# Splitting the broadcast of a block's softmax reciprocals into four transfers of one row each

## The chip, the core and the metric

The kernel runs on one core of a Trainium2 chip. A core has five instruction queues that run side by side and meet only through semaphores: TensorE (PE, matrix products, with its weight loads shown as PEld), VectorE (DVE), ScalarE (ACT), GpSimd (POOL) and SyncE (SP), which here does nothing but issue DMA transfers. Sixteen DMA engines carry the transfers. The metric is device time in microseconds; lower is better.

## The reference

One input x of 2048 rows and 512 columns is normalised row by row. The normalised xn goes through two branches, whose results are added to x: attention with 32 heads of width 16, and a gated feed-forward of inner width 1792.

```python
xn = layernorm(x)
q, k, v = split(xn @ wqkv)                      # 32 heads of width 16
scores = einsum("bhqd,bhkd->bhqk", q, k) * 16 ** -0.5
p = softmax(scores)                             # over the 2048 keys
a = einsum("bhqk,bhkd->bhqd", p, v) -> [2048, 512] @ wo
gate, up = xn @ W_gate, xn @ W_up
b = ((gate * (gate > 0)) * up) @ W_down
out = x + a + b
```

The softmax is not normalised before the product with v. The kernel forms exponentials, multiplies them with v and, in the same product, with a column of ones; that column gives each query's sum. The result is then multiplied by the reciprocal of the sum. The change concerns how these reciprocals reach the partitions where they are needed.

## The kernel before

**Blocks.** Attention runs in 32 blocks. A block is one group of 512 queries (`c4`, four of them), one group of eight heads (`gg`, four of them) and one half of that group (`ee`), so it holds four heads. Within a block the keys are taken in 16 tiles of 128. A product of keys and queries for a block's tile goes to PSUM; the exponential is taken either on ScalarE (L1418, two heads at a time, into `ring`) or, for the tiles marked in `QUAD_AT`, by an integer construction on VectorE and POOL (L1373, L1388, L1392, into `qd`). TensorE multiplies either with `v_aug` and adds the 16 tiles up in one PSUM bank. The feed-forward's products, the projections and the output rows are placed between the attention work.

**The end of a block** is the function `normalise`. The block's number is `n = 8 * c4 + 2 * gg + ee`; the last block has an ending of its own, so 31 blocks take this way:

1. VectorE copies the finished bank to `o_sb` (L1251; the very first block is summed in two parts, L1256). The four heads lie on 32 partitions each, and one of those partitions holds the sums of 512 queries.
2. SyncE issues the fetch of the four rows of sums, reshaped to 128 partitions of 16 (L1267, `rsum`, stream `n1`).
3. VectorE takes the reciprocal (L1268, `rrec`).
4. SyncE issues the write of the reciprocals to a scratch tensor in HBM, `rec_scr[n]`, four rows of 512 (L1269, stream `n2`).
5. SyncE issues the broadcast (L1272, `rb`, stream `n3`): row j of the scratch is read 32 times into partitions 32 j to 32 j + 31, in one transfer of 256 KB.
6. POOL multiplies `o_sb` by `rb` (L1280, or L1285 with four small transfers, L1289, that pack the second half's result into the place beside the first half's). The products with `wo` read the result, `oT`.

`rsum`, `rrec`, `rb` and `o_sb` each have two buffers, used in turn.

**Order.** Every engine's instructions stand in one fixed order. It was made ahead of time and is stored in the kernel as the compressed list `PLAN`; `Graph.run` reads it, and `Graph.emit` writes each engine's queue in that order and puts in the semaphore waits that the data flow requires. Nothing overtakes: when SyncE's next transfer waits for a semaphore, all transfers behind it wait too, and the same holds for a VectorE instruction that waits. Among what shares SyncE's queue with the steps above are slices of `qT` copied from `qf` (L892), slices of the feed-forward's weights (L1044), the rows of x for the residual (L1099), the stores of finished rows (L1118) and the packing transfers (L1289).

**Semaphores.** Each transfer belongs to a stream with a semaphore of its own, and adds 16 to it when it has landed. `emit` gives the transfer's consumers the value to wait for, `16 * (o.val + 1)`, where `o.val` counts earlier transfers of the stream; stream `n3` has four semaphores, used by the blocks in turn. At the end, SyncE waits for each stream's last value (`fin`).

## Time and profile before

| | us |
|---|---|
| median of three runs | 680.99 |
| lowest and highest | 680.63, 682.62 |
| the profiled execution, its own time | 681.0 |
| its span, from the first to the last instruction | 678.1 |

The granted TensorE clock is 1.000 throughout. HBM traffic is 26.35 MB read and 2.35 MB written, 42 GB/s over the span, and the transfers' packets took 17.3% of what sixteen DMA engines could give.

Views used below: the page's busy time of each engine; the chain of work that ended last, in order of time (start, length, what); timelines of one engine (start, length, instruction, and in brackets the idle time before it with what ended it); the view of one tile's instructions (duration in ns: min/median/max, then the first and last start); waits (who waited for whom: us in total, times, longest); and busy times of a stretch. A transfer's own instruction on SyncE, marked SPq, shows how long the *issue* took. The landing, where the profile knows it, stands apart as the time from issue to landing.

### The profile page before, as it was taken

What the parts mean: (1) busy time and instruction counts of PE and PEld (TensorE: products, weight loads), DVE (VectorE), ACT (ScalarE), POOL (GpSimd) and SP (SyncE); (2) the same over time, 40 slices, a digit from 0 to 9 for tenths busy, and PEclk for the clock granted to TensorE, in tenths of its full rate; (3) what the DMA queues carried; (4) which work ended last, traced back from release to release, by engine and by line L of the source; (5) the groups of instructions that cost most, each with busy time, mean ns of one, the idle gap of its engine ahead of it and who ended that gap; (6) DMA issues with size and microseconds to landing.
All of it is one profiled execution on the core that took longest, in us unless ns stands there. A gap on an engine that the chain in (4) does not pass through costs nothing.

```text
span 678.1 us, 46986 instructions
## 1 busy us (share of the span) xinstructions
PE 668.2 (99%) x22358; PEld 392.7 (58%) x21562; DVE 615.1 (91%) x1042; ACT 657.9 (97%) x718; POOL 511.7 (75%) x519
## 2 busy tenths in 40 slices
PE   8999999999999999989999999999999999999998
PEld 3555555566656666555555656555665565565554
DVE  9957899999999999889999989999999899999795
ACT  6999999999999999989999999999999999999995
POOL 3313657877788787888788878888888968888982
PEclk9999999999999999999999999999999999999999
DMA  7321221123121111111111112011112212101121
GB/s 218 66 50 29 60 68 44 47 66 93 47 85 35 48 28 54 39 47 47 51 49 34 52 30 59 17 40 40 58 28 73 61 33 72 39 23 38 33 64 58
DMA packets 55947, 35.97 MB, mean 53 GB/s; under 512 B 19336, under 2 KB 51784, under 8 KB 55752
## 3 DMA queue, kind: packets, MB, share of 16 engines
q1 hardware_dynamic: 55464, 32.71, 17.3%
q8 instruction: 171, 2.80, 1.7%
q10 hardware_dynamic: 288, 0.26, 0.1%
q14 instruction: 24, 0.20, 0.1%
HBM read 26.35 MB, written 2.35 MB: 42 GB/s over the span
## 4 chain that ended last, share of the span: by engine, by line
PE 91%; DVE 5%; DMA 2%; POOL 1%; issue 0%; SPq 0%; ACT 0%; DVEq 0%; POOLq 0%
PE ps L263 91%; DVE qd L1373 1%; DVE stats L758 1%; DVE xn_sb L771 1%; DMA rsum<-o_sb 1%; DMA xnT<-xn_sb 1%; POOL qd L1388 0%; DVE v_aug L909 0%; DMA rec_scr<-rrec 0%; DMA x_sb<-in_A_x_dram 0%; DVE qd L1392 0%; DVE qT L985 0%; DVE kT L902 0%; DVE mv L759 0%; DVE xnT L812 0%
## 5 line engine op out<-in xcount | busy, mean ns | idle before, releaser
L1418 ACT ACTIVATE ring<-ps 128x1024 bf16<-128x1024 f32 x706 | 651.4, 1079 | 6.2 <-PE ps L263 5.3
L1388 POOL TENSOR_TENSOR qd<-qd,ints 128x512 int32<-128x512 int32 x458 | 462.0, 1039 | 131.3 <-DVE qd L1392 81.0
L263 PE MATMUL ps<-qT,kT 64*32 64x512 bf16 x8192 | 466.6, 374 | 3.5 <-DVE qd L1373 2.4
L1373 DVE TENSOR_SCALAR qd<-ps 128x512 int16<-128x512 f32 x636 | 412.3, 684 | 36.2 <-PE ps L263 32.3
L263 PE MATMUL ps<-qd,v_aug 64*32 64x512 bf16 x3816 | 310.3, 375 | 0.1
L263 PE MATMUL ps<-ring,v_aug 64*32 64x512 bf16 x2824 | 244.2, 375 | 0.0
L1353 PEld LDWEIGHTS <-kT 64*32 64x32 bf16 x8032 | 170.9, 92 | 101.7 <-issue 15.5
L1325 PEld LDWEIGHTS <-v_aug 64*32 64x32 bf16 x6004 | 144.8, 92 | 71.8 <-issue 11.2
L263 PE MATMUL ps<-xnT,wgs 64*32 64x512 bf16 x1792 | 140.5, 374 | 0.2 <-DVE qd L1373 0.2
L263 PE MATMUL ps<-xnT,wus 64*32 64x512 bf16 x1792 | 137.3, 375 | 0.4 <-issue 0.2
L1392 DVE TENSOR_SCALAR qd<-qd 128x2048 int16<-128x2048 int16 x89 | 61.9, 701 | 1.2 <-PE ps L263 0.8
L842 PEld LDWEIGHTS <-wus 64*32 64x32 bf16 x1792 | 44.1, 91 | 23.7 <-issue 4.9
L842 PEld LDWEIGHTS <-wgs 64*32 64x32 bf16 x1792 | 43.2, 91 | 22.9 <-issue 3.8
L263 PE MATMUL ps<-Wd,hT 64*32 64x512 bf16 x608 | 55.3, 375 | 0.1
L842 PEld LDWEIGHTS <-hT 64*32 64x32 bf16 x1440 | 35.2, 92 | 21.1 <-issue 4.2
L263 PE MATMUL ps<-Wo_p,x_sb 64*32 64x512 bf16 x480 | 44.8, 375 | 0.0
L1057 DVE COPY up_sb<-ps 128x512 f32<-128x512 f32 x56 | 38.4, 686 | 3.4 <-PE ps L263 3.0
L263 PE MATMUL ps<-Wv,hT 64*32 64x512 bf16 x448 | 41.3, 375 | 0.0
L263 PE MATMUL ps<-Wv,xnT 64*32 64x512 bf16 x576 | 36.7, 374 | 0.5 <-DVE v_aug L909 0.3
L263 PE MATMUL ps<-xnT,Wq 64*32 64x512 bf16 x480 | 37.1, 375 | 0.0
L263 PE MATMUL ps<-xnT,Wk 64*32 64x512 bf16 x480 | 35.8, 374 | 0.3 <-DVE xnT L812 0.3
L263 PE MATMUL ps<-Wk,hT 64*32 64x512 bf16 x384 | 35.8, 375 | 0.0
(73 smaller groups left out, 306.5 us busy)
## 6 DMA issues: line engine op xcount, KB each, us to landing
rb<-rec_scr SPq DMA_DIRECT2D x31, 256.0 KB
wus<-in_B_W_up_dram SPq DMA_DIRECT2D x38, 128.0 KB, 2.9
wgs<-in_B_W_gate_dram SPq DMA_DIRECT2D x38, 128.0 KB, 2.7
xr_sb<-in_A_x_dram SPq DMA_DIRECT2D x16, 128.0 KB, 3.1
qT<-qf SPq DMA_DIRECT2D x120, 16.0 KB, 2.8
out_dram<-xn_sb SPq DMA_DIRECT2D x14, 128.0 KB, 3.2
x_sb<-in_A_x_dram SPq DMA_DIRECT2D x8, 128.0 KB, 2.8
x_sb<-oT SPq DMA_DIRECT2D x60, 16.0 KB, 3.0
```

The source lines that it names most:

```text
L263: return e.add_instruction(mybir.InstMatmult(name=e.bass.get_next_instruction_name(), engine=mybir.EngineType.PE, ins=[e.lower_ap(x), e.lo ...
L758: G.op("DVE", 580, lambda e, m=m: e.bn_stats(stats[:, m, :], xs(m)), reads=[t_xm[m]], writes=[t_st], prio=pr, order=last_xn if m == 4 else ())
L771: G.op("DVE", 320, lambda e, m=m, t=t_n: e.tensor_scalar(xn_sb[:, t.slot, :], xs(m), mv[:, m, 0:1], rstd[:, m:m + 1], op0=ALU.subtract, op ...
L842: e.ldweights(w()[rows, 32 * j:32 * j + 32], tile_position=(rows.start, 32 * j))
L1057: G.op("DVE", 603, lambda e: e.tensor_copy(up_sb[:, tup.slot, :], bank_of(tu)), reads=[tu], writes=[tup], prio=-590)
L1325: e.ldweights(vs(j), tile_position=(64 * half, 32 * j))
L1353: e.ldweights(ks(m), tile_position=(64 * half, 32 * m))
L1373: G.op("DVE", 601, lambda e, j=j, tx=tx: e.tensor_scalar(qd[:, tq.slot, 512 * j:512 * j + 512], ps[:, BANK[tx.slot], :], IBIAS[3], 0.0, op ...
L1388: G.op("POOL", POOL_NS / POOL_PIECES + 60, lambda e, x=x, n=n, c=slice(i * m, i * m + m): e.tensor_tensor(x().bitcast(I32)[:, c], raw().bi ...
L1392: G.op("DVE", 600, lambda e, n=n, x=x: e.tensor_scalar(x(), raw(), float(SHIFTS[n + 1]), None, op0=ALU.add), reads=[ti, tq], writes=[t], p ...
L1418: exp_ops[u] = G.op("ACT", 904, lambda e, tr=tr, k0=k0: e.activation(ring[:, tr.slot, :, :], ps[:, 4 * k0:4 * k0 + 2, :], ACTF.Exp, scale= ...
```

## The change

The broadcast of step 5 becomes a list of four transfers, one for each row j: `rec_scr[n, j]` to the 32 partitions from 32 j on, 64 KB each. They stand at the place in SyncE's order where the one transfer stood, one behind the other, and share its semaphore. The wait for `rec_scr` stands ahead of the first. Each piece adds 16 when it lands, so the value that consumers and the end of the kernel wait for on stream `n3` is 64 for a broadcast in place of 16. The order of all engines, every other transfer and all arithmetic stay as they were.

```diff
+PIECES = {"n3": 4}
...
                 if e == "SP":
-                    o.sem = (dsem[o.stream], 16 * (o.val + 1))
+                    o.sem = (dsem[o.stream], 16 * PIECES.get(o.stream[0], 1) * (o.val + 1))
...
-        fin = [(dsem[s], 16 * n) for s, n in streams.items()]
+        fin = [(dsem[s], 16 * PIECES.get(s[0], 1) * n) for s, n in streams.items()]
...
                 ins = o.fn(eng)
                 if e == "SP":
-                    ins.then_inc(o.sem[0], 16)
+                    for piece in ins if isinstance(ins, list) else [ins]:
+                        piece.then_inc(o.sem[0], 16)
...
-            dma(lambda e: e.dma_start(rb[:, trb.slot, :], rec_scr[n].unsqueeze(1).to_broadcast([4, 32, 512])), 520,
+            dma(lambda e: [e.dma_start(rb[32 * j:32 * j + 32, trb.slot, :], rec_scr[n, j:j + 1, :].to_broadcast([32, 512])) for j in range(PIECES["n3"])], 520,
                 reads=[tsc], writes=[trb], prio=pr - 50, stream=("n3", n % 4), name="n3")
```

## The prediction

> **What bounds the kernel now.** I began with the page: which engine is full, what the last chain consists of, and what the profile says of the broadcast's transfers.

> ```profile
> span 678.1 us, 46986 instructions
> PE 668.2 (99%) x22358; PEld 392.7 (58%) x21562; DVE 615.1 (91%) x1042; ACT 657.9 (97%) x718; POOL 511.7 (75%) x519
> PE 91%; DVE 5%; DMA 2%; POOL 1%; issue 0%; SPq 0%; ACT 0%; DVEq 0%; POOLq 0%
> ...
> rb<-rec_scr SPq DMA_DIRECT2D x31, 256.0 KB
> ...
> out_dram<-xn_sb ACTq DMA_DIRECT2D x2, 128.0 KB, 1.7
> ```

> TensorE is busy for 99% of the span and is 91% of the chain that ended last. A transfer can therefore matter only where it makes TensorE stand still, and the 2% of DMA in the chain is where to look. Note also that the 31 broadcasts have no time to landing in their row; what they take must be found in another way. The second view is the chain in order of time, around the only stretch after the start in which it leaves the compute engines for several microseconds.

> ```profile
> 282.45 2.74 DMA rec_scr<-rrec
> 285.21 0.58 SPq L1272
> 285.84 0.47 SPq L1118
> ...
> 286.35 4.72 DMA rsum<-o_sb
> ...
> 291.95 56.75 PE ps L263 x1763
> ```

> Here the broadcast of one block (L1272) is on the path by its issue: 0.58 us on SyncE's queue, then a store's issue, then the fetch of the **next** block's row sums (L1267), which takes 4.72 us to arrive. The timelines of VectorE and TensorE show what that costs:

> ```profile
> 288.28 0.68 DVE L1373 TENSOR_SCALAR qd<-ps 128x512 int16<-128x512 f32 x1
> 291.10 0.25 DVE L1268 RECIPROCAL rrec<-rsum 128x16 f32<-128x16 f32 x1 [2.14 <-DMA rsum<-o_sb]
> 291.95 0.38 PE L263 MATMUL ps<-qT,kT 64*32 64x512 bf16 x4 [1.98 <-DVE qd L1373]
> ```

> VectorE runs in a fixed order. The reciprocal waits 2.14 us for its row sums, the score patterns behind it (L1373) are late, and TensorE stands for 1.98 us. The same fetch with no broadcast ahead of it is much quicker; the two rows of another block, from SyncE's and VectorE's timelines, give a bound:

> ```profile
> 179.10 0.59 SPq L1267 DMA_DIRECT2D rsum<-o_sb  x1
> 181.41 0.24 DVE L1268 RECIPROCAL rrec<-rsum 128x16 f32<-128x16 f32 x1
> ```

> The reciprocal starts there 181.41 - 179.10 = 2.31 us after the fetch was issued, without waiting; so the fetch alone takes at most 2.31 us. Behind a broadcast it took 4.72. Why the broadcast holds it up is in the busy shares of two stretches (last two columns: share of the 16 DMA engines, GB/s), the second starting 1.65 us after a broadcast's issue:

> ```profile
> 402.75 0.58 SPq L1272 DMA_DIRECT2D rb<-rec_scr  x1
> ...
> 8.00:10.00 2.00, 1.92 (x49) 1.38 (x53) 2.00 (x6) 1.49 (x3) 0.00 (x0) 1.00 1.02 324
> 404.40:405.60 1.20, 1.20 (x56) 0.57 (x44) 0.88 (x3) 1.20 (x3) 1.20 (x2) 1.00 0.26 102
> ```

> During the opening loads all sixteen engines are busy and move 324 GB/s. While the broadcast is moving, the share is 0.26, which is 4.2 engines of 16, and the rate 102 GB/s. So the 256 KB (262,144 bytes) of one broadcast take about 262/102 = 2.57 us, on four engines. The excess of the late fetch, 4.72 - 2.31 = 2.4 us, is about that.

> **The change part by part.** *Data.* A piece is 64 KB, from one row to 32 partitions. If it runs on all sixteen engines at the opening's rate it takes 65.5/324 = 0.20 us. The fetch behind it then meets no queue worth counting, and I take it at 2.31 us, the bound above; the shorter end is 1.7, the quickest landing that any group of transfers shows on the page (the two stores from ScalarE's queue, whose row stands above), the longer end the 4.72 it has now.

> [...]

> *Issue.* SyncE issues four instructions instead of one. What they cost is bounded by the view of each tile's instructions (duration in ns, min/median/max):

> ```profile
> L1272 SPq DMA_DIRECT2D rb<-rec_scr x31: 528/578/598, 76.8 to 661.8; - x31
> L1267 SPq DMA_DIRECT2D rsum<-o_sb x31: 543/593/687, 58.7 to 656.2; - x31
> L1099 SPq DMA_DIRECT2D xr_sb<-in_A_x_dram x16: 336/472/1056, 73.1 to 662.4; - x16
> L892 SPq DMA_DIRECT2D qT<-qf x120: 507/584/1777, 40.8 to 638.2; - x120
> ```

> The nearest row is the load of xr_sb, also from HBM to SBUF in plain rows: median 0.47 us. With 0.04 us between issues (285.21 + 0.58 to 285.84 above leaves 0.05) four take 4 x 0.47 + 3 x 0.04 = 2.00 us in place of 0.58: **1.42 us more** of SyncE's queue. The ends are 4 x 0.34 + 0.12 = 1.48 (0.9 more) and 4 x 0.58 + 0.12 = 2.44 (1.9 more). But there is a catch in the last column. The broadcast and the row-sum fetch never took over 0.69 us to issue, while other kinds take up to 1.06 and 1.78 now and then. The pieces may join the kinds that can be held up. Around the spot that matters such an issue stands in SyncE's timeline:

> ```profile
> 286.99 0.76 SPq L1044 DMA_DIRECT2D wgs<-in_B_W_gate_dram  x1
> ```

> It is 0.3 us above the 0.47. I add one such delay, and take 1.42 + 0.3 = 1.7 us at the decisive place.

> *The place at 286.* The fetch goes out at 286.35 + 1.7 = 288.05 and its reciprocal starts at 288.05 + 2.31 = 290.36 instead of 291.10: 0.74 us earlier, and TensorE, which waits 1.98 us behind it, with it. With the ends above: 286.35 + 0.9 + 1.7 = 288.95 is before VectorE is free (288.28 + 0.68 = 288.96), so all of the 1.98 is gained; with 1.9 + 2.31 the gain is 0.54; and with 4.72 there is a loss.

> *The second place.* VectorE waits for row sums just once more: the first row, from the view of waits, gives the total, the number and the longest (us, times, us). The other four are from SyncE's and VectorE's timelines:

> ```profile
> DVE rrec L1268 <- DMA rsum<-o_sb: 2.5, 2, 2.1
> 515.59 0.58 SPq L1272 DMA_DIRECT2D rb<-rec_scr  x1
> 516.77 0.57 SPq L1267 DMA_DIRECT2D rsum<-o_sb  x1
> ...
> 520.30 0.68 DVE L1057 COPY up_sb<-ps 128x512 f32<-128x512 f32 x1
> 521.34 0.25 DVE L1268 RECIPROCAL rrec<-rsum 128x16 f32<-128x16 f32 x1 [0.36 <-DMA rsum<-o_sb]
> ```

> The pieces end at 515.59 + 2.0 + 0.3 = 517.9, the fetch is back by 517.9 + 0.04 + 2.31 = 520.25, before VectorE is free at 520.98. The 0.36 us goes; TensorE shows no wait beside it, so I count 0.1.

> *The consumer.* The multiply (L1280, L1285, on POOL) needs all four pieces. The last is issued 3 x 0.51 = 1.53 us after the first. Loads to x_sb land in 2.8 us at the median on the page's issue rows, those to xr_sb in 2.0 to 4.8. So rb is there 4.3 us after the first issue (3.5 to 6.3). The tightest use I found:

> ```profile
> 189.27 0.58 SPq L1272 DMA_DIRECT2D rb<-rec_scr  x1
> 194.17 1.28 POOL L1280 TENSOR_TENSOR x_sb<-o_sb,rb 128x512 bf16<-128x512 f32 x1
> x_sb<-in_A_x_dram SPq DMA_DIRECT2D x8, 128.0 KB, 2.8
> DMA to landing us min/median/max: 2.0/3.1/4.8
> ```

> That is 4.90 us, above 4.3. At the long end the multiply is 1.4 us late; POOL then uses up part of the idle time that it now spends waiting for VectorE. I count nothing.

> *Everything queued behind.* Thirty-one broadcasts add 31 x 1.42 = 44 us of issuing (53 with 1.7 each). Behind them in SyncE's order stand slices of qT, weight slices, stores and the next block's fetches. I cost their delay at nothing, because SyncE itself waits at most of these steps and so catches up:

> ```profile
> SPq L1269 <- DVE rrec L1268: 53.6, 15, 10.6
> POOL qd L1388 <- DVE qd L1392: 81.0, 61, 15.6
> ```

> The first of these waits alone is 53.6 us. Where no such wait stands between, as at 286, the cover is gone, and each microsecond of issue is a microsecond for what is behind.

> *Sum.* -0.74 - 0.1 = -0.8 us on the profiled execution's own 681.0 us (span 678.1, 2.9 around it), which is also the median of the three runs, 680.99. **Forecast 680.2 us.** A measurement of this kernel tells about 0.3%, 2.0 us, from no change; so the forecast is "no difference that can be told".

> **Rivals.** *Full gain.* The pieces issue at 0.34 to 0.43 us and no long one falls at 286: both waits vanish, -1.98 - 0.36 = -2.3, 678.7 us. For it speaks the minimum of the xr_sb row, against it that its median is 0.47.

> *SyncE's issues take over* (slower). The row sums are now behind four issues. The gain at 286 is used up once they take 291.10 - 2.31 - 286.35 = 2.4 us more than now, that is 0.72 us a piece: from there on the wait only grows. If all four take the 1.06 us of the xr_sb row's maximum, they need 4.36 us, 3.8 more; the reciprocal is at 286.35 + 3.8 + 2.31 = 292.46 (+1.36), and at the second place at 515.59 + 4.36 + 0.04 + 2.31 = 522.30 (+0.96): +2.3, and as much again if a further pair of blocks loses its cover: 683.3 to 685.6, say 684. For it: the maxima of three issue rows; against it: the medians, and SyncE's long waits.

> *The broadcast lands no sooner* (slower). Either the pieces stay on few engines, so that the change does not do what it says, or sixteen engines reading one 2 KB row get no more than the 102 GB/s of now. Then the fetch still takes 4.72 us and starts 1.42 to 1.9 later: +1.42 to 1.9 at 286, and at 516 the start moves by 0.8 to 1.3 (0.6 us of gap takes the rest): +2.2 to +3.2, 683.2 to 684.2. For it: no row here shows sixteen engines on one source row; against it: the first loads reach 324 GB/s.

> [...]

> **How the numbers follow.** Forecast 0.45 (its own range 679.4 to 681.5), full gain 0.17, SyncE's issues 0.25, no sooner landing 0.13. The range must reach the full gain below and the middle of both slower cases above: 678.7 to 684.6. Faster by over 0.3% (below 679.0) comes from the full gain, 0.17; slower from the two slow rivals less the share that stays under 683.0, 0.36; the rest, 0.47, is within.

> **What would show it.** In the changed kernel's profile the rows of L1272 should count 124, and now carry a time to landing near 2.8 us; the share of the DMA engines after a broadcast should be a short burst, no stretch of 0.26. Their median should be near 0.47 us, with some over 1. VectorE's wait for the row sums near 286 should fall from 2.14 to about 1.4 us, TensorE's from 1.98 to about 1.2, and the one at 521 vanish. I am wrong if new waits of TensorE appear behind a reciprocal, if POOL comes to wait for rb in many blocks, or if the chain shows SyncE's queue in more blocks than now.

## The result, and the profile after

| | us |
|---|---|
| before, median of 11 runs | 682.25 (678.39 to 684.23) |
| after, median of 11 runs | 677.22 (675.67 to 679.42) |
| after over before, 95% interval | 0.9938 (0.9918 to 0.9958) |
| the profiled execution after, its own time and its span | 677.22, 675.0 |

The changed kernel is 0.62% faster, about 4 us, where 0.8 us was forecast, and its time lies under the predicted range. Executions more than 1.5% above the fastest of the same kernel are left out of every ratio, mean and count below: three of 105 of the kernel before and one of its copy. The page of the profile after, its span, the busy times, the shares of the last chain and the row of the broadcast's transfers:

```profile
span 675.0 us, 47079 instructions
PE 666.8 (99%) x22358; PEld 389.3 (58%) x21562; DVE 615.3 (91%) x1042; ACT 656.7 (97%) x718; POOL 512.1 (76%) x519
PE 84%; ACT 6%; DVE 5%; DMA 2%; SPq 1%; issue 0%; POOL 0%
rb<-rec_scr SPq DMA_DIRECT2D x124, 64.0 KB, 2.2
```

There are 93 instructions more, three for each of 31 blocks. The broadcasts now have a time to landing, 2.2 us at the median for a piece. The chain still passes through one broadcast only, that of block 10. Its parts around there, in order of time (start, length, what):

```profile
282.09 1.86 DMA rec_scr<-rrec
...
283.97 0.33 SPq L1274
...
284.34 1.53 SPq L1274
...
285.92 0.43 SPq L1274
...
286.39 0.42 SPq L1274
...
286.85 0.42 SPq L1120
...
287.32 1.88 DMA rsum<-o_sb
```

Four issues stand where one stood, 0.33, 1.53, 0.43 and 0.42 us long. One of them was held up by 1.1 us; the forecast had put 0.3 us there for such a delay. The fetch of the next block's row sums then takes 1.88 us, not 4.72. VectorE's timeline and TensorE's view of waits (us in total, times, longest) show what is left of the wait:

```profile
289.22 0.25 DVE L1270 RECIPROCAL rrec<-rsum 128x16 f32<-128x16 f32 x1 [1.41 <-DMA rsum<-o_sb]
```

```profile
PE ps L264 <- DVE qd L1375: 1.4, 2, 1.2
```

VectorE's wait fell from 2.14 to 1.41 us, TensorE's from 1.98 to 1.24. The prediction also expected short bursts of all sixteen DMA engines. One piece stands alone in this stretch (busy times, then clock, share of the DMA engines, GB/s):

```profile
284.90:285.40 0.50, 0.50 (x28) 0.27 (x16) 0.30 (x1) 0.50 (x2) 0.00 (x0) 1.00 0.35 123
```

That is 62 KB in 0.5 us, at a mean of 5.6 engines' worth. It is a burst, and more than the 4.2 engines of the whole broadcast, but neither sixteen at a time (the highest share in any 0.05 us of it is 0.68, 10.9 engines) nor the 0.20 us that the prediction took for a piece.

At the second place nothing is left. SyncE's and VectorE's timelines there:

```profile
512.64 2.92 SPq L1274 DMA_DIRECT2D rb<-rec_scr  x4
515.60 0.60 SPq L1269 DMA_DIRECT2D rsum<-o_sb  x1
```

```profile
518.25 0.68 DVE L1059 COPY up_sb<-ps 128x512 f32<-128x512 f32 x1
518.85 0.24 DVE L1270 RECIPROCAL rrec<-rsum 128x16 f32<-128x16 f32 x1
```

The reciprocal follows the copy with no bracket behind it, so its row sums were there. The view of the tile `rb` (issue in ns, then POOL's idle time before its multiplies, then the landing):

```profile
L1274 SPq DMA_DIRECT2D rb<-rec_scr x124: 303/422/1762, 77.4 to 660.4; - x124
...
its engine sat idle before it (us, times) until:
  DVE qd L1394: 5.4, 5
...
DMA to landing us min/median/max: 1.9/2.2/3.6
```

POOL does not wait for `rb` at all in this execution. So the waits that the prediction gave for the place at 286 are in the profile, to within 0.1 us. One of its signs of being wrong is there as well: SyncE's queue is on the last chain at a second place, behind the broadcast that follows the one at 512.64. Two rows of the chain, and the wait of TensorE that ends it:

```profile
526.05 0.51 SPq L894
...
526.60 3.74 DMA x_sb<-oT
```

```profile
PE ps L264 <- DMA x_sb<-oT: 0.3, 1, 0.3
```

There a packing transfer is late, and it costs TensorE 0.3 us. The two profiles differ by 3.1 us of span, however, and 0.74 of that is the wait. The rest is what the experiments are about.

### The profile page after: what moved, and what is told of

Same layout as the page of the kernel before. It is cut to its first block, busy times and chain, and to the rows that moved or that the text cites. A ratio compares the mean times of both kernels' runs of the same rounds, so it can differ in the third digit from the quotient of the medians.

```text
span 675.0 us, 47079 instructions
## 1 busy us (share of the span) xinstructions
PE 666.8 (99%) x22358; PEld 389.3 (58%) x21562; DVE 615.3 (91%) x1042; ACT 656.7 (97%) x718; POOL 512.1 (76%) x519
## 4 chain that ended last, share of the span: by engine, by line
PE 84%; ACT 6%; DVE 5%; DMA 2%; SPq 1%; issue 0%; POOL 0%
PE ps L264 84%; ACT ring L1420 6%; DVE stats L760 1%; DVE qd L1375 1%; DVE xn_sb L773 1%; DMA x_sb<-oT 1%; DMA xnT<-xn_sb 1%; DVE v_aug L911 0%; SPq L1274 0%; SPq L1046 0%; DMA x_sb<-in_A_x_dram 0%; DMA rsum<-o_sb 0%; DMA rec_scr<-rrec 0%; DVE qT L987 0%; DVE kT L904 0%
## 5 line engine op out<-in xcount | busy, mean ns | idle before, releaser
L1355 PEld LDWEIGHTS <-kT 64*32 64x32 bf16 x8032 | 169.0, 92 | 102.4 <-issue 14.4
## 6 DMA issues: line engine op xcount, KB each, us to landing
wus<-in_B_W_up_dram SPq DMA_DIRECT2D x38, 128.0 KB, 2.8
wgs<-in_B_W_gate_dram SPq DMA_DIRECT2D x38, 128.0 KB, 2.5
xr_sb<-in_A_x_dram SPq DMA_DIRECT2D x16, 128.0 KB, 3.1
out_dram<-xn_sb SPq DMA_DIRECT2D x14, 128.0 KB, 1.9
x_sb<-in_A_x_dram SPq DMA_DIRECT2D x8, 128.0 KB, 2.5
```

Of the source, the lines that this page charges most:

```text
L1355: e.ldweights(ks(m), tile_position=(64 * half, 32 * m))
```

## The experiments

All times below are medians of the chip that ran the kernel, and ratios are against runs of the kernel before, of the same chip, with their 95% intervals. The kernel before took 686.44 us on the first chip, 687.5 on the second, 688.55 on the third and 687.26 on the fourth; differences are therefore taken within one chip only.

### Which of the 31 broadcasts matters

The first kernel splits the broadcasts of blocks 10 and 22 alone, those behind which the two waits stood. The second splits all but these two.

```diff
+            def spread(e):
+                if not whole:
+                    return [e.dma_start(rb[32 * j:32 * j + 32, trb.slot, :], rec_scr[n, j:j + 1, :].to_broadcast([32, 512])) for j in range(PIECES["n3"])]
+                return e.dma_start(rb[:, trb.slot, :], rec_scr[n].unsqueeze(1).to_broadcast([4, 32, 512]))
+            whole = n not in (10, 22)          # the second kernel: n in (10, 22)
```

> Only the broadcasts of blocks 10 and 22 go out as four pieces, the two behind which VectorE waited for the next block's row sums; the other 29 stay whole. If the whole gain of the change comes from these waits (theory W), this is as fast as the change: ratio to before 0.994. If only the part that the profile shows at that place comes from there (the shift of TensorE at 292 us in the two profiles, 0.73 us) and the rest from all broadcasts (theory F: while a broadcast holds four DMA engines for 2.6 us, instruction transfers for TensorE start late and it runs dry for 0.3 to 0.8 us now and then), the ratio is about 0.999 (-0.75 us).

> The complement: all broadcasts in four pieces except those of blocks 10 and 22. Theory W: no gain, ratio 1.000, and VectorE's 2.1 us wait near 289 us as in before. Theory F: the wait stays, yet most of the gain is there, ratio about 0.995 (-3.4 us), and TensorE's weight loads wait less for instructions (the 'issue' waits: 47 us in before, 44 with the change).

Two blocks: 683.91 us, ratio 0.996 (0.9937 to 0.9984). All others: 684.95 us, 0.9967 (0.9938 to 0.9996). Both gain, and neither gains all. The second kernel keeps both waits for the row sums and is faster than before nonetheless, so part of the gain seems to lie away from them; its interval ends just below 1, so this run alone does not prove it. Its profile showed something else. The view of waits, and then busy times around its second wait (the last three columns are the granted TensorE clock, the share of the DMA engines, GB/s):

```profile
DVE rrec L1270 <- DMA rsum<-o_sb: 5.1, 2, 2.8
PE ps L264 <- DVE qd L1380: 4.0, 3, 2.0
```

```profile
526.00:527.00 1.00, 0.00 (x0) 0.00 (x0) 0.62 (x2) 0.29 (x1) 0.76 (x1) 1.00 0.00 0
527.00:528.00 1.00, 0.77 (x20) 0.33 (x20) 0.77 (x2) 0.00 (x0) 1.00 (x2) 0.91 0.09 8
528.00:529.00 1.00, 1.00 (x24) 0.32 (x16) 0.55 (x1) 0.08 (x1) 0.51 (x1) 0.50 0.38 111
529.00:530.00 1.00, 1.00 (x32) 0.42 (x24) 0.83 (x3) 0.94 (x1) 0.00 (x0) 0.50 0.51 168
530.00:531.00 1.00, 1.00 (x32) 0.39 (x24) 0.61 (x2) 0.40 (x1) 0.00 (x0) 0.50 0.61 174
531.00:532.00 1.00, 1.00 (x40) 0.45 (x32) 0.46 (x1) 0.72 (x2) 0.00 (x0) 0.88 0.47 150
```

TensorE stands still for 1.97 us, starts again at 527.2, and then its clock is **halved** until about 531.2. The clock lost is 0.09 + 3 x 0.50 + 0.12 = 1.7 us, nearly as much as the wait itself. The wait at 292, of 1.86 us, has no such stretch behind it in this execution. The profiles of before and after could not show it: both ran at 1.000.

### The shape of the split

One kernel makes four transfers of 128 columns, each of all four rows to all 128 partitions: four pieces again, but on few engines (at block 10 its share of the DMA engines was 0.27 to 0.30, where the whole broadcast's was 0.26, in the stretch from 404.4 us on). The other makes eight pieces, half a row's partitions each.

```diff
-            dma(lambda e: [e.dma_start(rb[32 * j:32 * j + 32, trb.slot, :], rec_scr[n, j:j + 1, :].to_broadcast([32, 512])) for j in range(PIECES["n3"])], 520,
+            dma(lambda e: [e.dma_start(rb[:, trb.slot, 128 * j:128 * j + 128], rec_scr[n, :, 128 * j:128 * j + 128].unsqueeze(1).to_broadcast([4, 32, 128])) for j in range(PIECES["n3"])], 520,
```

```diff
-PIECES = {"n3": 4}
+PIECES = {"n3": 8}
...
+            dma(lambda e: [e.dma_start(rb[16 * j:16 * j + 16, trb.slot, :], rec_scr[n, j // 2:j // 2 + 1, :].to_broadcast([16, 512])) for j in range(PIECES["n3"])], 520,
```

> Four transfers per broadcast as in the change, but each takes 128 columns of all four rows, so that four rows stay outermost. If the number of engines is what counts (theories W and F both), the data still sits on four engines, the fetch of row sums still queues behind it and starts about 2 us later: slower than before by 2 to 4 us, ratio 1.003 to 1.006. If the gain came from several small transfers as such (theory S), it is as fast as the change, 0.994.

> [...] Expected: slower than the change by 2 us, ratio to before 0.997; and if SyncE's queue is near its limit in many blocks (the rival that I forecast), 1.003 or more.

Columns: 683.63 us, 0.9962 (0.9936 to 0.9988), a gain; the loss expected of it did not come. Its tile view, two of its waits, and SyncE's and VectorE's timelines at block 10:

```profile
L1274 SPq DMA_DIRECT2D rb<-rec_scr x124: 507/514/721, 77.8 to 666.8; - x124
```

```profile
DVE rrec L1270 <- DMA rsum<-o_sb: 2.7, 2, 1.4
PE ps L264 <- DVE qd L1375: 2.1, 3, 1.3
```

```profile
285.22 2.31 SPq L1274 DMA_DIRECT2D rb<-rec_scr  x4
...
288.09 0.56 SPq L1269 DMA_DIRECT2D rsum<-o_sb  x1
```

```profile
290.62 0.25 DVE L1270 RECIPROCAL rrec<-rsum 128x16 f32<-128x16 f32 x1 [1.44 <-DMA rsum<-o_sb]
```

The four issues take 2.31 us, so the fetch goes out 2.87 us after the first of them, where it went out 1.14 us after the whole broadcast. By then about half of the data has moved (69 GB/s over the 2.09 us from 286.0 on, 144 KB), at a share of the DMA engines of 0.27 to 0.30, and the fetch is answered within 290.62 - 288.09 = 2.53 us. The fetch is shorter largely because it starts later. Counted from the broadcast's first issue, the reciprocal starts 5.89 us later in before (291.10 - 285.21), 5.40 us here and 5.25 us in the kernel after (289.22 - 283.97). At block 10 the wait comes out at the same 1.4 us as with the pieces of one row, one of which ran at a share of 0.35. At block 22 it does not: the fetch takes up to 3.55 us there, and VectorE waits 1.23 us, where it waited 0.36 before and not at all after. TensorE's waits behind the patterns thus fell only from 2.6 to 2.1 us in all, and the kernel gained 3 us, so this run too points to a gain elsewhere.

Eight pieces: 709.35 us, 1.0328 (1.0284 to 1.0372), much slower. Its tile view and its waits:

```profile
L1274 SPq DMA_DIRECT2D rb<-rec_scr x248: 302/421/1948, 78.3 to 692.4; - x124
```

```profile
DVE rrec L1270 <- DMA rsum<-o_sb: 11.1, 4, 4.3
PE ps L264 <- DVE qd L1375: 10.2, 5, 4.0
POOL x_sb L1282 <- DMA rb<-rec_scr: 7.6, 6, 2.8
PE ps L264 <- POOL qd L1390: 4.9, 4, 1.9
```

This is the rival "SyncE's issues take over", as it was described: the fetch is late behind the issues in four blocks, POOL waits for `rb`, and TensorE waits for both. The issues of a broadcast now take 5.0 us of SyncE's queue in the mean, 4.4 us more than the whole one, against 1.75 us more with four pieces. The mean granted clock is also lower, 0.989 against 0.999, which is about 7 of the 22 us. With eight pieces this rival decides; with four it does not.

### Copies, and less data

On the second chip ran plain copies of the two kernels, the kernel after with the fetch of block 11's row sums moved ahead of block 10's broadcast, and the kernel before with the broadcast cut to 16 partitions from block 2 on (it leaves part of the normalisation undone). The move is made once the order has been read:

```diff
+        q = self.queue["SP"]
+        late = [o for o in q if o.stream[0] == "n1"][11]
+        to = q.index([o for o in q if o.stream[0] == "n3"][10])
+        q.remove(late)
+        q.insert(to, late)
+        for i, o in enumerate(q):
+            o.seq = i
```

> The kernel before, unchanged, as one of the kernels compared: its ratio tells what the comparison itself can tell, 1.000. Its profile is a second one of before, taken beside the other kernels of this call: if TensorE's waits for instructions differ between executions as much as between before and the change, the 44 against 47 us of 'issue' waits of its weight loads prove nothing; theory F wants more of them here than in the changed kernel of the same call.

> The changed kernel, unchanged, beside the others: 0.994 again if the first measurement holds (both theories). Theory F: TensorE's weight loads wait less on 'issue' than in the kernel before of this call.

> The changed kernel, with the fetch of block 11's row sums issued just ahead of block 10's broadcast in SyncE's order (its data had been ready for 9.8 us in before). VectorE's wait at 289 us in the changed kernel (1.41 us) and TensorE's behind it (1.24 us) go. Both theories: 1.2 us faster than the change, ratio to before 0.992. If what is left of the gain came through this wait in some other way (theory W), it is no faster than the change.

> From block 2 on the broadcast reaches 16 of the 128 partitions only, in one transfer of 32 KB from four rows; the rest of rb keeps an earlier block's values, so this part of the normalisation is left out. Neither engines are held nor issues added: what holding four engines for 2.6 us costs in all. Theory W: -2.0 us, TensorE's wait at 290 us, ratio 0.997. Theory F: that and the late instruction transfers, 0.991 to 0.993.

| kernel | median, us | ratio | interval |
|---|---|---|---|
| copy of before | 686.24 | 0.9985 | 0.9956 to 1.0013 |
| copy of after | 683.15 | 0.9947 | 0.9925 to 0.9970 |
| after, fetch moved | 683.22 | 0.9936 | 0.9909 to 0.9962 |
| 16 partitions | 680.95 | 0.9918 | 0.9888 to 0.9948 |

The gain repeats. Taking away the 1.2 us that TensorE still waits, by the move, changes the time of the split kernel by less than can be told here. The 16 partitions keep the whole broadcast's single issue and gain 0.8%. The copies also show how far one profile may be trusted. A first suspicion was that TensorE's instructions arrive earlier in the kernel after, since its weight loads waited less for "issue" there. Of the two kernels and their two copies, the largest such row (us in total, times, longest):

```profile
PEld L842 <- issue: 20.5, 76, 2.4
```

```profile
PEld L844 <- issue: 19.3, 79, 1.7
```

```profile
PEld L842 <- issue: 21.2, 73, 2.6
```

```profile
PEld L844 <- issue: 25.7, 86, 1.6
```

In the order before, after, copy of before, copy of after: the copy of the faster kernel has the most. Between two executions this wait differs by more than between the kernels, so 3.1 us of difference between two profiles proves nothing about it. In the copy of before, by the way, TensorE's wait was longer than in the profile of the prediction:

```profile
PE ps L263 <- DVE qd L1373: 2.6, 3, 2.3
```

### The waits taken away from both sides

Now the fetches of the row sums of blocks 11 and 23 go ahead of the broadcasts of blocks 10 and 22 in the kernel before (whole broadcast), in the kernel after (four pieces), and in the one with 16 partitions. None of these three then waits for row sums, so what is left between the first two is the split's effect elsewhere. The move is the one above for `n` in (10, 22). A fourth kernel has the whole broadcast and behind each one a second transfer of the same 256 KB to memory, so that twice the bytes move:

```diff
+                if n > 0:
+                    e.wait_ge(G.spare, 16 * n)
+                e.dma_start(spare[n], rec_scr[n].unsqueeze(1).to_broadcast([4, 32, 512])).then_inc(G.spare, 16)
```

> The kernel before with whole broadcasts; only the fetches of row sums of blocks 11 and 23 are moved ahead of the broadcasts of blocks 10 and 22, so VectorE no longer waits behind a whole broadcast. Theory W (the whole gain is these waits, which cost more in a usual execution than the 2.0 us of the one profiled): as fast as the change or faster, ratio to before 0.992 to 0.994. Theory F (four engines held, late instruction transfers): only part, 0.997.

> [...] Theory W: the same as w_whole, since nothing is left to gain; if the 1.75 us of added issue for each broadcast cost anything, slower than it. Theory F: 0.4% faster than w_whole, ratio to before 0.993.

> The same move with broadcasts that from block 2 on reach 16 partitions only (that part of the normalisation is left out): no waits, no engines held, no issues added. Theory W: the same as w_whole. Theory F: 0.4% faster than w_whole, 0.992 to 0.993.

> The same move with whole broadcasts, and behind each a second transfer of the same size and shape to an unused place in HBM, for which only the next such transfer waits: four engines are held for 5.2 us instead of 2.6. Theory F: as much slower than w_whole as that is slower than w_small, 0.4% or more, ratio to before about 1.001. Theory W: the same as w_whole unless the profile shows a new wait for a transfer queued behind the doubled one.

| kernel, with the move | median, us | ratio | interval |
|---|---|---|---|
| whole broadcast | 684.11 | 0.9942 | 0.9921 to 0.9963 |
| four pieces | 682.03 | 0.9910 | 0.9877 to 0.9944 |
| 16 partitions | 682.46 | 0.9920 | 0.9890 to 0.9950 |
| second transfer behind each | 699.86 | 1.0180 | 1.0150 to 1.0210 |

**Removing the waits alone**, with the broadcast left whole, gains 0.58%, 4 us, though TensorE waited 2.0 us in the profile before. With the split on top the mean time falls by another 2.6 us (standard error 0.7), and with 16 partitions by 2.0 (0.7): the split gains here about as much as leaving out most of the broadcast's data. It is not free even so. In the profile of the four pieces with the move POOL waits 1.3 us for `rb` once and TensorE 0.8 us for a packing transfer, and SyncE's queue is on the last chain at both places; with the whole broadcast and the move it is nowhere on it.

The second transfer costs 16 us, so more of the same traffic is dear. The run does not tell by what, since each second transfer also takes time to issue on SyncE's queue (0.64 us for the one in the profile of the late fetch, below) and writes 256 KB to HBM. In its profile VectorE waits for row sums again in spite of the move, TensorE's weight loads wait longer for "issue", and one new wait of 2.7 us is for a slice of `qT`. The row by itself is the first one's counterpart with the whole broadcast and the move:

```profile
PEld L1370 <- issue: 28.9, 90, 3.0
...
DVE rrec L1279 <- DMA rsum<-o_sb: 2.9, 2, 1.7
PE ps L263 <- DMA qT<-qf: 2.7, 1, 2.7
```

```profile
PEld L1361 <- issue: 21.2, 79, 0.8
```

Behind the wait for `qT`, from 538 to 541 us, the clock is again near one half (0.51, 0.50 and 0.50 in these three), as behind the wait of the first group.

### Does the wait cost the clock?

The mean granted clock of every execution tells whether such a stretch fell into it: one that loses 1.7 us is 0.25% of the span, so I count an execution at 1.000 or 0.999 as without one, and one at 0.998 or less as with it.

| kernel | executions | mean clock | executions at 0.999 or more |
|---|---|---|---|
| before, on the four chips | 102 | 0.9986 | 53 |
| after, its copy, two blocks split | 35 | 0.9998 | 35 |
| whole broadcast with the move | 24 | 0.9995 | 24 |
| four pieces with the move | 18 | 0.9997 | 18 |
| 16 partitions, without and with the move | 12 | 0.9997 | 12 |
| after, block 11's fetch moved | 12 | 0.9994 | 10 |
| columns | 12 | 0.9995 | 11 |
| columns with the move | 7 | 0.9994 | 6 |
| all but two blocks split | 12 | 0.9983 | 4 |
| second transfer behind each | 6 | 0.9967 | 1 |
| eight pieces | 6 | 0.9888 | 0 |
| late fetch (below) | 12 | 0.9962 | 0 |

Within one chip, the executions of before that lost the clock took 2.6, 2.4, 0.8 and 0.8 us longer in the mean than those that kept it; weighted by their errors that is 1.7 us (standard error 0.4), as the lost clock alone would give.

Some of these rows are from the last group. In it the wait is made longer, by one more transfer of 256 KB behind block 10's broadcast, ahead of block 11's fetch:

```diff
+                if n == 10:
+                    e.dma_start(spare[:], rec_scr[n].unsqueeze(1).to_broadcast([4, 32, 512])).then_inc(G.spare, 16)
```

Beside it ran the whole broadcast and the four pieces with the move once more, and the four transfers of columns with the move.

> The kernel before with one more transfer of the same 256 KB, to memory, right behind the broadcast of block 10 and ahead of the fetch of block 11's row sums; the product is unchanged. If a standstill of TensorE of some 2 us or more can halve its granted clock for a stretch (clock 0.50 at 528 to 531 us in the kernel with all but two blocks split, and at 539 to 541 us in the kernel with the second transfer everywhere), the wait at 289 us grows from 2.0 us to about 4.5 us and every execution loses the clock once: mean granted clock at most 0.998 in all of them (before: about half of them at 1.000), and the time is 2.5 us (the longer wait) plus about 1 us (the clock in the other half of the executions) above before, 3 to 4.5 us in all. If the clock has nothing to do with the wait, the clocks are spread as in before and the time is 2 to 2.6 us above it.

> The kernel before with the fetches of the row sums of blocks 11 and 23 issued ahead of the broadcasts of blocks 10 and 22, once more, beside its neighbours on another chip. It has no wait of DVE for the row sums, so what the kernel with the four pieces and the same move gains over it is the gain away from those waits. If the waits and the clock that they cost explain the whole gain of the change, this kernel and the split one agree within 0.15%; if the split also gains elsewhere, this one is 2 to 3 us slower than the split one.

> The same move in the kernel after. If all of the gain is the wait and its clock: within 0.15% of the kernel with the whole broadcast and the move. If the four pieces also gain elsewhere, by letting TensorE's instructions and other transfers through: 2 to 3 us faster than it (0.3 to 0.45%). Mean granted clock 0.9995 or more in both cases.

> The same move, with the broadcast in four transfers of 128 columns of all four rows to all 128 partitions (64 KB each, the same four DMA engines, 5 us in all). If what gains away from the waits is that other DMA engines carry the pieces, nothing is gained here over the whole broadcast (within 0.15%). If it is that four short transfers stand in place of one long one, whichever engines carry them, this is as fast as the pieces of one row, 2 to 3 us below the whole broadcast. If nothing is gained away from the waits, all three agree.

| kernel | median, us | ratio | interval |
|---|---|---|---|
| late fetch | 689.88 | 1.0045 | 1.0019 to 1.0071 |
| whole broadcast, move | 683.29 | 0.9941 | 0.9917 to 0.9965 |
| four pieces, move | 682.68 | 0.9929 | 0.9903 to 0.9956 |
| columns, move | 681.41 | 0.9915 | 0.9885 to 0.9945 |

With the late fetch, TensorE waits 4.47 us, and every one of twelve executions lost the clock, some of them by more than one such stretch (lowest 0.994). TensorE's timeline and the clock behind the wait:

```profile
297.26 0.38 PE L263 MATMUL ps<-qT,kT 64*32 64x512 bf16 x4 [4.47 <-DVE qd L1381]
```

```profile
297.00:298.00 1.00, 0.74 (x20) 0.39 (x20) 1.00 (x3) 0.00 (x0) 0.23 (x1) 0.76 0.09 8
298.00:299.00 1.00, 1.00 (x32) 0.49 (x17) 0.45 (x2) 0.43 (x1) 1.00 (x2) 0.50 0.00 0
299.00:300.00 1.00, 1.00 (x32) 0.71 (x24) 0.80 (x2) 0.59 (x1) 1.00 (x2) 0.50 0.14 8
300.00:301.00 1.00, 1.00 (x28) 0.75 (x20) 0.53 (x1) 0.73 (x1) 1.00 (x2) 0.53 0.22 84
301.00:302.00 1.00, 1.00 (x48) 0.45 (x36) 0.71 (x2) 0.72 (x2) 1.00 (x1) 1.00 0.26 100
```

Again 0.24 + 0.50 + 0.50 + 0.47 = 1.7 us of clock are lost. The theory had asked for a clock of at most 0.998 in all executions and 3 to 4.5 us; the clock came out so, and the mean is 2.9 us up (standard error 0.65), at the low end and not apart from the other theory's 2 to 2.6. The clock, not the time, decides here, together with the opposite edit: where the fetch is moved ahead, without the second transfer, 64 of 67 executions keep it, against 53 of 102 before. The other three (two of the kernel after with block 11's fetch moved, one of the columns with the move) say that something else can cost the clock too; their own traces are not on record.

The second question, whether the split gains away from the waits, got a weaker answer. Four pieces against the whole broadcast, both with the move: -2.6 us on the third chip, -1.05 on the fourth (means, standard errors 0.7 and 0.8), together -1.9, with a 95% interval of about -2.9 to -0.8. The columns stand at -1.95 (0.7) against the same neighbour. So the split gains one to three microseconds elsewhere, and the number of engines does not seem to matter for it, since the columns gain as well, at a share of 0.27 to 0.30 where a piece of one row showed 0.35.

## Why the prediction was wrong

**What held.** TensorE was the bound, and the one place that set the end was the fetch behind block 10's broadcast. The step "290.36 instead of 291.10", a gain of 0.74 us, was met in its size: VectorE waited 1.41 us (about 1.4 forecast), TensorE 1.24 (about 1.2). That it came out so well is partly luck, since the terms under it erred in opposite directions: the issues took 2.84 us in place of 0.58, 2.26 more and not 1.7, because the one hold-up was 1.1 us and not 0.3; and the fetch took 1.9 us and not the bound of 2.31. A piece's data took some 0.5 us and not 0.20, which changed nothing; that a piece runs on all sixteen engines, on which the 0.20 rests, no run shows: the one looked at had a mean share of 0.35, 5.6 engines. The second wait vanished as forecast. The landing of a piece, 2.2 us, was below the 2.8 taken from loads of x, and POOL's wait for `rb`, counted at nothing, was nothing in that execution (1.2 us in two blocks in the copy). The use that the prediction called the tightest it found, 4.90 us, was not the tightest: in the profile before POOL already waits 1.13 us for `rb` at 452.31. The extra issues, 1.75 us a block in the mean over the 31, were counted at nothing and cost TensorE 0.3 us that the view of waits shows.

**What failed** is the **sum**: "-0.74 - 0.1 = -0.8 us on the profiled execution's own 681.0 us". It priced TensorE's standstill by its length in one execution, and it put at nothing, as a possible loss only, what the change does to everything else queued. Three things were outside of it:

- *The clock.* In the profile with all but two blocks split, a standstill of 1.97 us was followed by some 3.4 us at half clock. Of the kernel before, 49 of 102 executions lost clock, with a mean of 0.9986 over all; after, none of 23 (after and its copy), with 0.9997. The difference of 0.0011 over 680 us is 0.75 us on the mean. (The 102 ran on the chips of the experiments; for the eleven runs of before in the result no clock is on record but that of the profiled one.) The profiled execution ran at 1.000, so neither its span nor any row of it could show this.
- *The standstill itself varies*: 1.98 us in the profile of before, 2.31 in its copy; after, 1.24 and 0.9 (in the copy, by its view of waits). That makes the gain 0.7 to 1.4 us where 0.74 was taken.
- *Elsewhere.* The prediction had "everything queued behind" only as a possible loss, of SyncE's time. With no wait for row sums on either side the split still gains some 1.9 us (0.8 to 2.9).

Together 0.75 + 1.05 + 1.9 = 3.7 us from the terms' middles, with 2.3 and 5.1 us from their ends, and the copies differ by 3.7 us in their means (683.6 for the copy of after, 687.3 for the kernel before and its copy on that chip, standard error 0.6). So the gain is accounted for within what the runs can tell, though the terms come from different kernels and chips and their agreement to 0.1 us is chance. Of the three, the first is shown by edits both ways, the second rests on two profiles of each kernel, and the third is measured without its cause being known.

**The rivals.** *Full gain* came nearest in time, but not for its reason: the issues were not all short, and 1.4 us of the wait stayed. *SyncE's issues take over* was wrong for four pieces and right for eight, where the ratio is 1.033. *The broadcast lands no sooner* is refuted by the fetch, 1.88 us for 4.72. Nor would its condition have been enough: the columns stay on few engines (0.27 to 0.30, against 0.26 for the whole broadcast) and gained all the same.

**What stays open** is what the gain elsewhere consists of. The second transfer behind each broadcast lengthened TensorE's waits for "issue" (28.9 against 21.2 us in the largest row), so late instruction transfers (the page's queue of that kind moved 2.80 MB) are a candidate; but in the two kernels themselves these waits differ more from one execution to the next than between the kernels, and no run separates them from delays of other transfers, such as the slices of `qT`.

Of the versions that compute all, those with a split broadcast and the two fetches moved ahead have the lowest ratios: four pieces 0.991 and 0.993 on two chips, the columns 0.9915 on one of them. Against the kernel after (0.994 and 0.995) the difference is within the intervals.

## What to carry to other kernels

Price a standstill of the engine that sets the end by more than its length: look at the granted clock of many executions, not of the profiled one, before calling a wait of 2 us worth 2 us. Where a small fetch stands behind a large transfer on one queue, the first thing to try is to issue the fetch earlier, which cost no extra instruction here and gained 0.58% by itself; splitting the large transfer in four, with 1.75 us of added issue each time, gained 0.4 to 0.6%, and in eight, with 4.4 us, it lost 3.3%. Where between them the turn lies was not measured. A gain of 3 us in 680 cannot be read off two profiles, since two executions of one kernel differ by more: the kernel after and its copy had spans of 675.0 and 685.5 us, on two chips.
